# Fourier transform and feed-forward layer: the rounded products read their columns in turn from two halves

## The chip, the core and the metric

The kernel runs on one NeuronCore of a Trainium2 chip. Its engines work at the same time, each through its own list of instructions: TensorE (PE) multiplies matrices, VectorE (DVE), ScalarE (ACT) and GpSimd (POOL) work element by element, and SyncE (SP) starts transfers. They wait for each other by semaphores. SBUF is the memory on the chip, PSUM the small memory that TensorE writes its sums to; both have 128 partitions. The metric is the time of one run on the device in microseconds.

## The reference

```python
X = np.fft.fft(x, axis=1)          # x: (8, 3072, 256), real
X = np.fft.fft(X, axis=2)
x = X.real.astype(np.float32).reshape(8 * 3072, 256)
h = x @ w_in                       # (256, 2048)
g = np.maximum(h, 0.0) + alpha * np.minimum(h, 0.0)
out = g @ w_out                    # (2048, 256)
```

A transform along both axes of each of eight batches, its real part, and then a layer of 2048 features with a leaky slope for each feature, and a second layer back to 256.

## The kernel before

The feature transform is folded into the first layer's weights, and symmetries of the real transform leave half of the columns (frequencies) to compute: two output rows, i = 0 and 1, are made from each. In what follows a column is a frequency, and the features lie on the partitions.

**Products.** The bulk of the work is `nc.tensor.matmul`: a stationary operand of 128 x 128 weights, and a moving operand whose columns pass through the array. To keep float precision with a fast product, most operands are split in two rounded floats (`F32R`): hi, the rounded value, and lo, what is left. A product of such numbers is then three: hi x hi, hi x lo, lo x hi. A few products at the start (the weights, the transform's units, and the second layer of block 0 for the first 14 feature groups) are taken in plain `F32`; the profile shows two records for each of these.

**Blocks and steps.** The columns are cut in 26 blocks (`BLOCKS`): 18 of 512 columns for the batches 1 to 6, and eight of 384 or 386 for the first and last batch. Each block runs through 16 steps, one for each group of 128 features. A step `step(s)` issues, in this order on TensorE:

- `ffn1(s + 3)` (L663 to L665): two sums q = 0, 1 of three products each, moving operand `X` (the transform's result, hi and lo side by side), into two of the four PSUM banks of the ring `pq`.
- `ffn2(s)` (L742): the second layer of the step three earlier, 12 products with the moving operands hi and lo of `g`, into the four banks `acc`, which collect over the 16 steps of a block.

Beside them, `pair(s + 3)` turns the first layer's sums into the second layer's operands:

- L681, VectorE: `pf` = the sum q = 0 plus a row (frequency 128 of the features, `xbc`, loaded once a block) times a weight for each feature.
- L688, VectorE: `d` = `pf` minus or plus the sum q = 1, for the two rows i.
- L692, ScalarE: `d` times the slope, written over the sum in PSUM.
- L646, VectorE: the larger of the two, which also ends the use of the bank in `pq`.
- L648, ScalarE, and L650, GpSimd: the split of `d` into hi and lo.

**Transform.** For each next batch, `fold_piece` (L369, on GpSimd and VectorE) folds the loaded rows, spread over the steps. Then `unit` (L524, plain floats) and `dft_odd` (L480, 36 rounded products of 384 columns in a batch through `dft_parts`) multiply with cosine tables, and `to_x` writes `X`. The table of `dft_odd` is split once in six pieces by `parts` (L472, L473).

**Order.** Nothing is planned at run time: the order on each engine is that of the calls. At the end of a block `evacuate` copies the four banks `acc` to SBUF, and a transfer takes them out; the host puts the columns in their places.

## Time and profile before

| what | value |
|---|---|
| median of 3 runs | 1768.83 us (1768.09 to 1771.08) |
| the profiled execution, its span | 1770.41 us, 1768.6 us |
| TensorE busy | 1754.7 us, 99% |
| VectorE, GpSimd, ScalarE busy | 83%, 74%, 62% |
| mean granted clock of TensorE | 0.998 |
| data moved | 71.35 MB, 40 GB/s |

The span reaches from the first to the last instruction; the profiled execution's own time also holds what lies around it. A granted clock of 1.00 is the upper of TensorE's two levels, 2.4 GHz; the lower is 1.2 GHz. In the views, a matmul's record lasts longer than the distance to the next one, since products overlap in the array: distances are read from start to start. "x12" in a row of the chain or of the timeline means 12 instructions merged into one row.

### The profile page before, as it was taken

Reading aid. Unit: us, or ns where it says so; the run is one execution under the profiler, and the core shown is the slowest. Engines: PE = TensorE matmul, PEld = TensorE weight load, DVE = VectorE, ACT = ScalarE, POOL = GpSimd, SP = SyncE. Lnnn points to the kernel's source line nnn. Section 1 sums busy time; section 2 is a strip of 40 time slices with the busy share of each in tenths; the row PEclk is TensorE's granted clock in tenths of the full one; section 3 lists DMA queues with packets and bytes.
Section 4 is the critical chain, followed back from the end, with each engine's and each line's share of the span. In section 5 each row is a group of like instructions: output and inputs, shape, how many; then the busy total and the mean of one; then the engine's idle time right before and its main releaser. Section 6 shows DMA issues by size and latency. Waiting matters only on the chain.

```text
span 1768.6 us, 25521 instructions
## 1 busy us (share of the span) xinstructions
PE 1754.7 (99%) x8222; PEld 1498.3 (85%) x8222; DVE 1468.3 (83%) x2545; ACT 1105.4 (62%) x2029; POOL 1309.0 (74%) x1349
## 2 busy tenths in 40 slices
PE   8999999999999999999999999999999999999999
PEld 6789998888888888888888888888888888899998
DVE  8978987888778887888878888788877888778886
ACT  6866676555666566665665556655666556666665
POOL 2379887888678876788777887778877788666665
PEclk9999999999999999999999999999999999999999
DMA  6411120011000010010100101001100010000000
GB/s 234 147 35 44 41 67 19 19 54 49 18 31 37 31 66 1 31 48 30 55 24 7 66 13 54 24 8 65 37 30 25 18 43 29 1 29 23 23 19 19
DMA packets 26152, 71.35 MB, mean 40 GB/s; under 512 B 6272, under 2 KB 8354, under 8 KB 25890
## 3 DMA queue, kind: packets, MB, share of 16 engines
q1 hardware_dynamic: 25266, 69.27, 11.1%
q8 instruction: 64, 1.05, 0.2%
q14 instruction: 70, 0.57, 0.1%
q10 hardware_dynamic: 752, 0.45, 0.1%
HBM read 44.45 MB, written 25.25 MB: 39 GB/s over the span
## 4 chain that ended last, share of the span: by engine, by line
PE 98%; DVE 1%; POOL 0%; issue 0%; ACT 0%; DVEq 0%; POOLq 0%; ACTq 0%
PE acc L742 59%; PE pq L663 10%; PE pq L664 10%; PE pq L665 10%; PE ps L524 3%; PE ps L480 2%; PE acc L729 2%; PE ps L301 1%; PE fold L378 0%; POOL w L270 0%; PE warm L610 0%; DVE d L688 0%; DVE wm L261 0%; DVE pf L681 0%; DVE we L257 0%
## 5 line engine op out<-in xcount | busy, mean ns | idle before, releaser
L650 POOL TENSOR_TENSOR lo<-d,hi 128x512 fp32r<-128x512 f32 (+2 forms) x804 | 979.8, 1239 | 344.3 <-ACT hi L648 333.9
L648 ACT ACTIVATE hi<-d 128x512 fp32r<-128x512 f32 (+2 forms) x804 | 484.4, 603 | 486.3 <-DVE d L646 338.2
L646 DVE SCALAR_TENSOR_TENSOR d<-d,sg,pq 128x512 f32<-128x512 f32 (+2 forms) x804 | 565.1, 703 | 3.2 <-ACT pq L692 1.9
L692 ACT ACTIVATE pq<-d,sga 128x512 f32<-128x512 f32 (+2 forms) x804 | 520.3, 648 | 47.6 <-DVE d L688 47.6
L688 DVE TENSOR_TENSOR d<-pf,pq 128x512 f32<-128x512 f32 (+2 forms) x832 | 529.6, 639 | 7.8
L742 PE MATMUL acc<-hi,woh 128*128 128x512 f32 (+2 forms) x1608 | 478.1, 378 | 0.0
L681 DVE SCALAR_TENSOR_TENSOR pf<-xbc,w,pq 128x512 f32<-128x512 f32 (+2 forms) x416 | 293.2, 705 | 191.2 <-PE pq L665 188.1
L742 PE MATMUL acc<-hi,wol 128*128 128x512 f32 (+2 forms) x1608 | 418.6, 379 | 0.0
L742 PE MATMUL acc<-lo,woh 128*128 128x512 f32 (+2 forms) x1608 | 418.4, 379 | 0.0
L742 PEld LDWEIGHTS acc<-lo,woh 128*128 128x128 f32 x1608 | 297.5, 188 | 52.9
L742 PEld LDWEIGHTS acc<-hi,woh 128*128 128x128 f32 x1608 | 299.2, 188 | 50.2
L742 PEld LDWEIGHTS acc<-hi,wol 128*128 128x128 f32 x1608 | 297.8, 188 | 51.7
L663 PE MATMUL pq<-X,wih 128*128 128x512 f32 (+2 forms) x832 | 321.6, 387 | 3.3 <-DVE d L646 2.6
L664 PE MATMUL pq<-X,wih 128*128 128x512 f32 (+2 forms) x832 | 313.2, 376 | 0.2 <-DVE X L573 0.2
L665 PE MATMUL pq<-X,wil 128*128 128x512 f32 (+2 forms) x832 | 312.8, 376 | 0.0
L663 PEld LDWEIGHTS pq<-X,wih 128*128 128x128 f32 x832 | 156.6, 188 | 30.1 <-DVE d L646 4.0
L665 PEld LDWEIGHTS pq<-X,wil 128*128 128x128 f32 x832 | 156.8, 188 | 26.1 <-DVE wil L318 0.2
L664 PEld LDWEIGHTS pq<-X,wih 128*128 128x128 f32 x832 | 157.3, 189 | 24.4 <-DVE X L573 0.4
L573 POOL TENSOR_TENSOR X<-y,X 128x384 fp32r<-128x384 f32 (+3 forms) x67 | 63.9, 966 | 28.9 <-ACT X L572 28.7
L369 POOL TENSOR_TENSOR raw<-raw 128x512 f32<-128x512 f32 (+2 forms) x84 | 70.4, 838 | 0.0
L541 DVE TENSOR_TENSOR y<-ps,os 128x192 f32<-128x192 f32 (+3 forms) x76 | 23.5, 352 | 48.4 <-ACT os L531 48.4
L270 POOL TENSOR_TENSOR w<-we,wm 128x512 int32<-128x512 int32 x16 | 20.5, 1279 | 50.5 <-DVE wm L261 28.6
(155 smaller groups left out, 979.6 us busy)
## 6 DMA issues: line engine op xcount, KB each, us to landing
raw<-in_xh SPq DMA_DIRECT2D x46, 512.0 KB
out<-o SPq DMA_DIRECT2D x36, 512.0 KB
raw<-in_w SPq DMA_DIRECT2D x15, 512.0 KB
xbc<-xcd SPq DMA_DIRECT2D x18, 256.0 KB
out<-o SPq DMA_DIRECT2D x10, 386.0 KB
out<-o SPq DMA_DIRECT2D x6, 384.0 KB
odd<-in_odd SPq DMA_DIRECT2D x1, 1152.0 KB
table<-in_odd SPq DMA_DIRECT2D x6, 192.0 KB
```

The source lines that it names most:

```text
L369: yield size, lambda o=o, i0=i0, i1=i1, op=op: e.tensor_tensor(out=o, in0=i0, in1=i1, op=op)
L573: lo_engine.tensor_tensor(out=lo, in0=v, in1=hi.bitcast(F32), op=ALU.subtract)
L646: V.scalar_tensor_tensor(out=d, in0=d, scalar=sg[:, f:f + 1], in1=ad, op0=ALU.mult, op1=ALU.max)
L648: S.activation(out=hi, in_=d, func=ACTF.Copy)
L650: G.tensor_tensor(out=lo, in0=d, in1=hi.bitcast(F32), op=ALU.subtract)
L663: nc.tensor.matmul(out=t_, lhsT=wih[:, f, q], rhs=xh, start=True, stop=False)
L664: nc.tensor.matmul(out=t_, lhsT=wih[:, f, q], rhs=xl, start=False, stop=False)
L665: nc.tensor.matmul(out=t_, lhsT=wil[:, f, q], rhs=xh, start=False, stop=True)
L681: V.scalar_tensor_tensor(out=pf, in0=xbc[g], scalar=w128[:, f:f + 1], in1=ps[0], op0=ALU.mult, op1=ALU.add,)
L688: V.tensor_tensor(out=d, in0=pf, in1=ps[1], op=ALU.add if i else ALU.subtract)
L692: S.activation(out=ad, in_=d, func=ACTF.Copy, scale=sga[:, f:f + 1])
L742: nc.tensor.matmul(out=acc[o, i], lhsT=wt[:, f, o * P:(o + 1) * P], rhs=hl[i][part], start=(f == 0 and n[o] == 0), stop=(f == KF - 1 and n ...
```

## The change

Every product of rounded floats now reads its moving operand in another order: column 0, column n/2, column 1, column n/2 + 1 and so on, for n columns. The output is written to consecutive places of the PSUM bank, as before, so the sums stand there in this turned order. Two small helpers say so: `_halves` names the source in turn from its two halves, `_pairs` names the destination as consecutive pairs.

- First layer: `X` is read in turn, and the sums stand in turned order. The row `xbc` is read in turn by L681, so that it matches.
- Second layer, blocks 1 to 25: hi and lo, which stand in turned order, are read in turn once more. Block 0 stays as it is, since most of its products are plain floats. The host puts the columns back (`_turn`, once for block 0 and twice for the others).
- Odd transform: the two parts of the cosine table are written in SBUF in the inverse order, so that reading in turn gives the old order of its sums.

No instruction of computation is added, removed or moved, and no transfer. Plain-float products are as before.

```diff
+def _turn(n):
+    return np.arange(n).reshape(2, n // 2).T.reshape(-1)
+
+def _halves(v):
+    return v.rearrange("p (h a) -> p a h", h=2)
+
+def _pairs(v):
+    return v.rearrange("p (a h) -> p a h", h=2)
...
             hi, lo = (v_[:, at:at + n] for v_ in split_in[key])
+            if key == "odd":
+                v = v.rearrange("p q (a h) -> p (q a) h", h=2)
+                hi, lo = (v_.rearrange("p q (h a) -> p (q a) h", h=2) for v_ in (hi, lo))
...
-                nc.tensor.matmul(out=ps, lhsT=lhsT, rhs=rhs, start=(i == 0), stop=(i == n - 1))
+                nc.tensor.matmul(
+                    out=_pairs(ps), lhsT=lhsT, rhs=_halves(rhs), start=(i == 0), stop=(i == n - 1),
+                )
...
-            nc.tensor.matmul(out=t_, lhsT=wih[:, f, q], rhs=xh, start=True, stop=False)
-            nc.tensor.matmul(out=t_, lhsT=wih[:, f, q], rhs=xl, start=False, stop=False)
-            nc.tensor.matmul(out=t_, lhsT=wil[:, f, q], rhs=xh, start=False, stop=True)
+            xh, xl, out = _halves(xh), _halves(xl), _pairs(t_)
+            nc.tensor.matmul(out=out, lhsT=wih[:, f, q], rhs=xh, start=True, stop=False)
+            nc.tensor.matmul(out=out, lhsT=wih[:, f, q], rhs=xl, start=False, stop=False)
+            nc.tensor.matmul(out=out, lhsT=wil[:, f, q], rhs=xh, start=False, stop=True)
...
-                out=pf, in0=xbc[g], scalar=w128[:, f:f + 1], in1=ps[0], op0=ALU.mult, op1=ALU.add,
+                out=_pairs(pf), in0=_halves(xbc[g]), scalar=w128[:, f:f + 1], in1=_pairs(ps[0]),
+                op0=ALU.mult, op1=ALU.add,
...
+                out, rhs = acc[o, i], hl[i][part]
+                if g:
+                    out, rhs = _pairs(out), _halves(rhs)
                 nc.tensor.matmul(
-                    out=acc[o, i], lhsT=wt[:, f, o * P:(o + 1) * P], rhs=hl[i][part],
+                    out=out, lhsT=wt[:, f, o * P:(o + 1) * P], rhs=rhs,
```

What the built program has beyond that is waits: 384 semaphore instructions more on TensorE and 377 more on ScalarE. On TensorE, in the middle of the program, the second of a step's two first-layer sums waited for VectorE alone (a name after "waits" is the engine whose semaphore is waited for):

```order
L663 MATMUL pq<-X,wih 128x512 [waits DVE_49]
L664 MATMUL pq<-X,wih 128x512
L665 MATMUL pq<-X,wil 128x512
L663 MATMUL pq<-X,wih 128x512 [waits DVE_49]
L664 MATMUL pq<-X,wih 128x512
L665 MATMUL pq<-X,wil 128x512
```

The same place of TensorE in the changed program, whose line numbers are 21 higher there:

```order
L684 MATMUL pq<-X,wih 128x512 [waits DVE_49]
L685 MATMUL pq<-X,wih 128x512
L686 MATMUL pq<-X,wil 128x512
L684 MATMUL pq<-X,wih 128x512 [waits DVE_49,PE_49]
L685 MATMUL pq<-X,wih 128x512
L686 MATMUL pq<-X,wil 128x512
```

The products stand as before; the fourth now also waits for TensorE's own product of some 34 products earlier, the one that wrote this bank last.

## Rows read from the trace of the kernel before

**Rows 1.** The page: TensorE's busy time, and the chain that ended last by line.
```profile
PE 1754.7 (99%) x8222; PEld 1498.3 (85%) x8222; DVE 1468.3 (83%) x2545; ACT 1105.4 (62%) x2029; POOL 1309.0 (74%) x1349
...
PE acc L742 59%; PE pq L663 10%; PE pq L664 10%; PE pq L665 10%; PE ps L524 3%; PE ps L480 2%; PE acc L729 2%; PE ps L301 1%; PE fold L378 0%; POOL w L270 0%; PE warm L610 0%; DVE d L688 0%; DVE wm L261 0%; DVE pf L681 0%; DVE we L257 0%
```

**Rows 2.** Waits of TensorE: total us, times, longest.
```profile
PE pq L663 <- DVE d L646: 2.6, 4, 1.2
```

**Rows 3.** Chain of waits, steady steps: start us, us, what.
```profile
1170.72 2.80 PE acc L742 x12
...
1174.90 2.80 PE acc L742 x12
```

**Rows 4.** The same view where an odd transform stands between two layers.
```profile
287.75 3.14 PE ps L480 x18
290.89 0.24 PE pq L663
```

**Rows 5.** Timeline of TensorE at the end: start us, us, instruction; six products between.
```profile
1762.28 0.52 PE L742 MATMUL acc<-hi,wol 128*128 128x386 f32 x2
...
1763.34 0.52 PE L742 MATMUL acc<-hi,wol 128*128 128x386 f32 x2
```

**Rows 6.** Timeline of TensorE at the start, and that stretch's busy times and clock.
```profile
41.02 0.53 PE L665 MATMUL pq<-X,wil 128*128 128x386 f32 x1
...
42.31 3.40 PE L729 MATMUL acc<-gw,whole 128*128 128x386 f32 x8
...
40.00:42.30 2.30, 2.30 (x11) 2.30 (x10) 2.30 (x5) 2.21 (x5) 0.11 (x2) 0.54 0.73 228
```

**Rows 7.** Timeline of TensorE in block 0: plain-float products and what follows them.
```profile
65.59 2.76 PE L729 MATMUL acc<-gw,whole 128*128 128x386 f32 x8
68.19 1.05 PE L301 MATMUL ps<-w,feat 128*128 128x128 f32 x8
```

**Rows 8.** Groups by line and form: count | busy us, mean ns | idle before.
```profile
L742 PE MATMUL acc<-hi,woh 128*128 128x512 f32 x1152 | 360.9, 394 | 0.0
...
L663 PE MATMUL pq<-X,wih 128*128 128x512 f32 x576 | 230.3, 400 | 0.0
...
L742 PE MATMUL acc<-hi,woh 128*128 128x386 f32 x264 | 68.2, 339 | 0.0
...
L663 PE MATMUL pq<-X,wih 128*128 128x386 f32 x160 | 56.3, 352 | 1.0 <-ACT X L572 0.5 <-DVE d L646 0.5
...
L742 PE MATMUL acc<-hi,woh 128*128 128x384 f32 x192 | 49.0, 337 | 0.0
...
L663 PE MATMUL pq<-X,wih 128*128 128x384 f32 x96 | 34.9, 364 | 2.2 <-DVE d L646 2.1
...
L480 PE MATMUL ps<-oddh,col 128*128 128x384 f32 x42 | 14.1, 336 | 0.0
```

**Rows 9.** Timeline of VectorE in a steady step; idle time before in brackets.
```profile
1003.50 0.75 DVE L681 SCALAR_TENSOR_TENSOR pf<-xbc,w,pq 128x512 f32<-128x512 f32 x1 [0.57 <-PE pq L665]
1004.16 0.74 DVE L646 SCALAR_TENSOR_TENSOR d<-d,sg,pq 128x512 f32<-128x512 f32 x1
...
1006.08 0.68 DVE L688 TENSOR_TENSOR d<-pf,pq 128x512 f32<-128x512 f32 x1
1007.68 0.75 DVE L681 SCALAR_TENSOR_TENSOR pf<-xbc,w,pq 128x512 f32<-128x512 f32 x1 [0.92 <-PE pq L665]
```

**Rows 10.** Windows: a batch; us, then PE, PEld, DVE, ACT, POOL busy, PEclk, DMA.
```profile
1137.94:1350.49 212.55, 212.55 (x935) 173.91 (x935) 176.55 (x285) 130.25 (x225) 164.84 (x162) 1.00 0.10 34
```

**Rows 11.** Groups by line and form on VectorE; columns as in rows 8.
```profile
L681 DVE SCALAR_TENSOR_TENSOR pf<-xbc,w,pq 128x512 f32<-128x512 f32 x288 | 214.7, 745 | 145.7 <-PE pq L665 143.9
...
L681 DVE SCALAR_TENSOR_TENSOR pf<-xbc,w,pq 128x384 f32<-128x384 f32 x48 | 29.2, 609 | 8.8 <-PE pq L665 8.0
...
L257 DVE SCALAR_TENSOR_TENSOR we<-raw,we 128x512 int32<-128x512 int32 x15 | 10.3, 684 | 0.0
```

## The prediction, made before the changed kernel was run

> **What bounds the kernel now.** I read the page first, then the chain of waits, then TensorE alone in order of time, then VectorE beside it.

> The page says that TensorE is busy 99% of the span, and the chain that ended last is TensorE almost throughout: the second layer's rounded products (L742) hold 59%, the first layer's (L663 to L665) 30%, the odd transform (L480) 2% [rows 1]. The waits of TensorE are nearly nothing: the largest that the loop shows is 2.6 us in all [rows 2]. So there is no wait to remove. The time is the number of products times the time of one, and the reader should ask what one costs.

> A product's own duration (0.39 us) is no price, since the next begins before it ends; the price is from start to start. In the chain of waits a steady step of a 512-column block begins its second-layer products at 1170.72 and again at 1174.90: these 12 and the 6 of the first layer in 4.18 us, 232.2 ns each [rows 3]. At 2.4 GHz, the higher of the clock's two levels, 512 columns at one a clock would be 512 / 2.4 = 213.3 ns. The granted clock is 1.00 there [rows 10]. So 18.9 ns, 8.9%, is lost in every product.

> Three more readings say what kind of loss this is.
> - It grows with the columns. 18 products of 384 columns take 3.14 us, 174.4 ns each [rows 4], against 160.0: 14.4 ns, 9.0%. A price per product would have been 18.9 ns again.
> - It isn't another engine's traffic. At the very end six products of 386 columns take 1.06 us, 176.7 ns each against 160.8 [rows 5], 9.9%, when the other engines have little or nothing left to read.
> - It goes when columns are asked for at half the rate. At a granted clock of 0.54 (practically the lower level) four first-layer products of 386 columns take 1.29 us, 322.5 ns each; 386 / 1.2 is 321.7 [rows 6]. The unrounded products of block 0 at full clock take 2.59 us for eight records of 386 columns, 323.8 ns each: two clocks a column are 321.7, and 2.1 ns is left over [rows 7].

> So the array follows its clock whenever a 4-byte column is due every 0.83 ns, and falls behind, by the same share in every stage, when one is due every 0.42 ns. Either the moving operand's columns can't be fetched at that rate as they are fetched now, or the array can't take rounded columns at that rate. The change bears on the first alone: same products, same results, same instructions, another order of addresses.

> **The change part by part.** It touches 7548 products [rows 8]: 5184 of 512 columns (576 x 3 of the first layer, 1152 x 3 of the second), 1248 of 386 (160 x 3, and 264 x 3 less the 24 of block 0, which stay in order), and 1116 of 384 (96 x 3, 192 x 3, 42 x 6 of the odd transform).

> *What one product may become.* Nothing in this trace reads a moving operand with a long step between neighbouring columns, so I bound it. Best: the loss goes but for the 2.1 ns that a product keeps where columns come slowly [rows 7]: 215.4 ns for 512, 163.0 for 386, 162.1 for 384. Worst: each column takes two clocks, as in [rows 7]: 428.8, 323.8 and 322.1 ns. Between lies no change. The best end saves 5184 x 16.8 = 87.1, 1248 x 13.7 = 17.1 and 1116 x 12.3 = 13.7 us, 118 us together. The worst end adds 5184 x 196.6 + 1248 x 147.1 + 1116 x 147.7 = 1368 us.

> I take the best end. The loss is a fixed share of the columns, gone at half the demand and untouched by the neighbours: that looks like one run of addresses asked for faster than the place that holds it can answer. Two runs in turn, 1024 bytes apart at 512 columns, ask each place half as often, and half as often is what [rows 6, 7] show to be free.

> [...]

> *VectorE's sum of the first layer* (L681, 416 times) now reads its row vector from two halves in turn. The nearest row is L257: 512 words at a step of two words, 684 ns [rows 11], no longer than L646's 0.74 us on consecutive words [rows 9]. So I take nothing; the other end is each element at twice L681's own slope, (745 - 609) / 128 = 1.06 ns an element [rows 11]: 0.75 us becomes about 1.3.

> *Does VectorE keep up?* In a steady step it starts its sum at 1003.50, ends its last operation at 1006.08 + 0.68 = 1006.76 and starts again at 1007.68 [rows 9]. A step shortened to 18 x 215.4 ns = 3.88 us leaves 0.6 of those 0.9 us. Over a batch of 48 steps it works 176.5 of 212.55 us [rows 10]; TensorE would need 212.55 less 864 x 16.8 ns and 36 x 12.3 ns, 197.6 us. VectorE then stands at 89%, GpSimd (164.8) at 83%. In single steps VectorE has more (two evacuation copies, a fold operation), but its first release for the next products comes 1004.16 + 0.74 = 1004.90, 1.8 us before they start at about 1006.7. For such steps and the start I add 5 us.

> *The added waits.* 384 first-layer products wait for an earlier product of TensorE too. It stands about 34 products back, some two steps or 7 us, so it is long done; what is added is one more semaphore instruction a step in the sequencer, and the chain shows no sequencer time of TensorE. Nothing. 377 more such instructions on ScalarE fall on an engine with 130 of 212.55 us of work [rows 10]. Nothing. The table's six splits write in turn on ScalarE and GpSimd, off the path. Nothing.

> *Sum.* The profiled execution took 1770.4 us, its span 1768.6: 1.8 us outside. 1768.6 - 117.9 + 5 = 1655.7 us of span, 1657.5 with what lies around it. That execution is 1.6 us above the median of the runs (1768.83), so on the median's scale **1656 us**.

> **The rivals.**
> - *Half the loss, or VectorE takes over: 1710 us.* If two runs in turn heal only half of the loss, the saving is 59 us. The same time comes another way: with L681 at 1.3 us VectorE would need 176.5 + 48 x 0.53 = 202 us of every batch and with its gaps some 205, past TensorE's 197.6; half of the 15 us that a batch gains is lost. For it: a fixed share can have two causes. Against: L257's row.
> [...]
> - *The array itself is the limit: 1769 us.* Rounded columns at full clock cost what they cost, wherever they lie. For it: the loss is the same share for both layers' operands and the transform's. Against: nothing in the trace separates it; that it vanishes at the lower clock fits it too.

> **How the numbers follow.** The full gain has 0.42, the half gain 0.22, no effect 0.12; slower has 0.24, of which I give 0.18 to a cost far above 1800 us and 0.06 to a small one. A measurement of this kernel tells 0.2% (3.5 us) from no change. So faster 0.64, same 0.12, slower 0.24. The likeliest case alone would lie within 1646 to 1672. The range from 1645 to 1780 takes in the first three cases and the start of the slow one, and leaves out the large slowdown: 0.2.

> **What would show it.** Right: a step of 512 columns lasts about 3.88 us in the chain, the 18 products of the odd transform 2.92 us instead of 3.14, the unrounded products and the cold stretch stay as they are, and L681 stays at 0.75 us. Half: steps of 4.0 us; if TensorE then waits for VectorE's L646 it was VectorE, and if not, the fetch. [...]

## The result, and the profile after

| | before | after |
|---|---|---|
| median | 1768.46 us (4 runs) | 1662.79 us (4 runs, 1659.61 to 1664.33) |
| ratio of the runs | | 0.940, 95% interval 0.938 to 0.942 |
| span of the profiled execution | 1768.6 us | 1662.5 us |

The four runs of the kernel before are the three of its table and one more. The change makes the kernel 6.0% faster. 1656 us was forecast.

The page of the changed kernel: busy times, and the chain that ended last by line (L767 is what L742 was, L684 to L686 are the first layer, L498 the odd transform).

```profile
PE 1642.7 (99%) x8222; PEld 1475.8 (89%) x8222; DVE 1473.8 (89%) x2545; ACT 1123.8 (68%) x2029; POOL 1299.3 (78%) x1349
...
PE 93%; DVE 4%; issue 1%; ACT 0%; DMA 0%; POOL 0%; DVEq 0%; SPq 0%; POOLq 0%; ACTq 0%
PE acc L767 56%; PE pq L684 10%; PE pq L685 10%; PE pq L686 10%; PE ps L544 3%; PE ps L498 2%; PE acc L751 2%; DVE d L710 1%; DVE pf L702 1%; PE ps L316 1%; DVE d L666 1%; PE fold L393 0%; DMA raw<-in_xh 0%; DVE wm L276 0%; DVE we L272 0%
```

Where [rows 1] had hardly anything but TensorE, 4% of the chain is VectorE now. The other engines work nearly as long as before (VectorE 1473.8 us against 1468.3, ScalarE 1123.8 against 1105.4); the span around them is shorter.

The chain of waits of the changed kernel, in steady steps and at an odd transform, answers [rows 3, 4]:

```profile
284.30 2.92 PE ps L498 x18
287.22 0.22 PE pq L684
...
1102.38 2.59 PE acc L767 x12
...
1106.26 2.59 PE acc L767 x12
```

A step lasts 3.88 us where it lasted 4.18: 12 products in 2.59 us are 215.8 ns each. 18 products of 384 columns take 2.92 us, 162.2 ns. The end of the kernel, in the timeline of TensorE, answers [rows 5]; eight products begin between these two rows:

```profile
1656.30 0.49 PE L767 MATMUL acc<-hi,wol 128*128 128x386 f32 x2
...
1657.61 0.49 PE L767 MATMUL acc<-lo,woh 128*128 128x386 f32 x2
```

163.8 ns each in place of 176.7. All three widths now stand 2 to 3 ns above one column a clock at 2.4 GHz (213.3, 160.0, 160.8). Taken as one column a clock, the runs bear this figure out: from 384 to 512 columns the price rises by 53.6 ns, 0.419 ns a column or 2.39 columns in a nanosecond, and at a granted clock of 0.50 four products of 386 columns take 1.29 us (below), 1.20 columns in a nanosecond.

What did not change: the plain-float products of block 0, eight records in 2.60 us, answer [rows 7]. Nor did the products at the lower clock (granted 0.50 from 41.17 to 42.46 us): four in 1.29 us in the turned order, as in [rows 6] in the plain one. The rows of both:

```profile
63.30 2.76 PE L751 MATMUL acc<-gw,whole 128*128 128x386 f32 x8
65.90 1.05 PE L316 MATMUL ps<-w,feat 128*128 128x128 f32 x8
```

```profile
41.17 0.53 PE L686 MATMUL pq<-X,wil 128*128 128x386 f32 x1
...
42.46 3.64 PE L751 MATMUL acc<-gw,whole 128*128 128x386 f32 x8
```

A batch in the windows (columns as in [rows 10]), and VectorE's sum by form (as in [rows 11]):

```profile
1073.20:1271.10 197.90, 197.90 (x936) 174.72 (x935) 176.88 (x284) 132.59 (x225) 163.37 (x162) 1.00 0.11 37
```

```profile
L702 DVE SCALAR_TENSOR_TENSOR pf<-xbc,w,pq 128x512 f32<-128x512 f32 x288 | 218.5, 759 | 66.0 <-PE pq L686 62.9
```

The batch was forecast at 197.6 us. TensorE never stands still in it, though VectorE is busy 89%. L702 costs 759 ns in place of 745, and VectorE's idle time before it has fallen from 145.7 us to 66.0: VectorE has that much less in reserve.

The waits of TensorE (total us, times, longest) show what is new:

```profile
PE pq L684 <- DVE d L666: 6.5, 9, 2.3
...
PE pq L685 <- POOL X L911: 1.8, 1, 1.8
```

The first was 2.6 us [rows 2]. Its longest, 2.30 us, stands in the first batch behind a fold operation on VectorE, of the kind that the 5 us of the forecast were meant for:

```profile
180.45 3.52 DVE L384 TENSOR_TENSOR xev<-raw 128x512 f32<-128x512 f32 x1 [0.20 <-DMA raw<-in_xh]
...
185.08 0.43 PE L684 MATMUL pq<-X,wih 128*128 128x384 f32 x1 [2.30 <-DVE d L666]
```

The second did not exist before, and the timeline of the changed kernel shows it in block 0:

```profile
60.15 0.41 PE L684 MATMUL pq<-X,wih 128*128 128x386 f32 x1
...
61.00 1.26 POOL L285 TENSOR_TENSOR w<-we,wm 128x512 int32<-128x512 int32 x1 [2.21 <-DVE wm L276]
...
62.20 0.13 POOL L911 MEMSET X<- 128x28 f32 x1
...
62.38 0.43 PE L685 MATMUL pq<-X,wih 128*128 128x386 f32 x1 [1.83 <-POOL X L911]
```

A product waits for the clearing of seven columns of `X`, which stands behind GpSimd's work on the weights. The product reads columns 0 to 385, the clearing is at 1537: they share nothing. But with the turned order the built program lets the clearing wait for TensorE and the product for the clearing. It is the first layer's order that does it: in `e8_second_only` below, where the first layer reads `X` in plain order, this wait is not in the list.

### The profile page after: what moved, and what is told of

The parts are those of the page before. It is cut to its first block, busy times and chain, and to the rows that moved or that the text cites. A ratio compares the mean times of both kernels' runs of the same rounds, so it can differ in the third digit from the quotient of the medians.

```text
span 1662.5 us, 26282 instructions
## 1 busy us (share of the span) xinstructions
PE 1642.7 (99%) x8222; PEld 1475.8 (89%) x8222; DVE 1473.8 (89%) x2545; ACT 1123.8 (68%) x2029; POOL 1299.3 (78%) x1349
## 4 chain that ended last, share of the span: by engine, by line
PE 93%; DVE 4%; issue 1%; ACT 0%; DMA 0%; POOL 0%; DVEq 0%; SPq 0%; POOLq 0%; ACTq 0%
PE acc L767 56%; PE pq L684 10%; PE pq L685 10%; PE pq L686 10%; PE ps L544 3%; PE ps L498 2%; PE acc L751 2%; DVE d L710 1%; DVE pf L702 1%; PE ps L316 1%; DVE d L666 1%; PE fold L393 0%; DMA raw<-in_xh 0%; DVE wm L276 0%; DVE we L272 0%
## 5 line engine op out<-in xcount | busy, mean ns | idle before, releaser
L714 ACT ACTIVATE pq<-d,sga 128x512 f32<-128x512 f32 (+2 forms) x804 | 526.3, 655 | 48.9 <-DVE d L710 48.1
L767 PE MATMUL acc<-hi,woh 128*128 128x512 f32 (+2 forms) x1608 | 454.1, 364 | 0.0
L767 PE MATMUL acc<-lo,woh 128*128 128x512 f32 (+2 forms) x1608 | 393.1, 364 | 0.0
L767 PE MATMUL acc<-hi,wol 128*128 128x512 f32 (+2 forms) x1608 | 393.1, 364 | 0.0
L702 DVE SCALAR_TENSOR_TENSOR pf<-xbc,w,pq 128x512 f32<-128x512 f32 (+2 forms) x416 | 298.3, 717 | 92.6 <-PE pq L686 87.6
L767 PEld LDWEIGHTS acc<-hi,woh 128*128 128x128 f32 x1608 | 298.0, 189 | 31.0
L767 PEld LDWEIGHTS acc<-lo,woh 128*128 128x128 f32 x1608 | 295.3, 189 | 30.9
L767 PEld LDWEIGHTS acc<-hi,wol 128*128 128x128 f32 x1608 | 295.3, 189 | 30.9
L684 PE MATMUL pq<-X,wih 128*128 128x512 f32 (+2 forms) x832 | 310.7, 373 | 7.1 <-DVE d L666 6.5
L685 PE MATMUL pq<-X,wih 128*128 128x512 f32 (+2 forms) x832 | 302.6, 364 | 2.0 <-POOL X L911 1.8
L686 PE MATMUL pq<-X,wil 128*128 128x512 f32 (+2 forms) x832 | 302.5, 364 | 0.0
L684 PEld LDWEIGHTS pq<-X,wih 128*128 128x128 f32 x832 | 157.6, 189 | 26.9 <-PE pq L686 4.1
L686 PEld LDWEIGHTS pq<-X,wil 128*128 128x128 f32 x832 | 157.6, 189 | 15.7 <-DVE wil L333 0.3
```

Source lines behind the costliest of these rows:

```text
L684: nc.tensor.matmul(out=out, lhsT=wih[:, f, q], rhs=xh, start=True, stop=False)
L685: nc.tensor.matmul(out=out, lhsT=wih[:, f, q], rhs=xl, start=False, stop=False)
L686: nc.tensor.matmul(out=out, lhsT=wil[:, f, q], rhs=xh, start=False, stop=True)
L702: V.scalar_tensor_tensor(out=_pairs(pf), in0=_halves(xbc[g]), scalar=w128[:, f:f + 1], in1=_pairs(ps[0]), op0=ALU.mult, op1=ALU.add,)
L714: S.activation(out=ad, in_=d, func=ACTF.Copy, scale=sga[:, f:f + 1])
L767: nc.tensor.matmul(out=out, lhsT=wt[:, f, o * P:(o + 1) * P], rhs=rhs, start=(f == 0 and n[o] == 0), stop=(f == KF - 1 and n[o] == 2),)
```

## The experiments

The result leaves open why the order heals. Theory A: a column must not lie in the same 16 bytes as the one before it. Theory B: two runs far apart are needed. That 16 bytes is the size that counts was an assumption at this point; `e2_near16` and `e9_near8` bear on it. The first four runs change the order in the 18 blocks of 512 columns alone: `_halves` and `_pairs` get another pattern there, and the host puts the columns back accordingly. The narrow blocks and the odd transform stay in turn from two halves. Each later cut of `_halves` shows its line against the first run's; `_pairs` follows it, so that the output of each product stays in consecutive places, and so does the host's `_turn`, but for `e7_each_twice`. In `e2_near16`, `e3_lines`, `e6_twos`, `e7_each_twice` and `e9_near8` the sum on VectorE reads its row in plain order, so the row is not at its columns there; the products are as many and as large as before. From each run the steady step in the chain of waits is shown: twelve products of the second layer, and the next twelve 18 products later.

**A step of 16 bytes** (`e1_step4`).

```diff
 def _halves(v):
+    if v.shape[-1] == WM:
+        return v.rearrange("p (a h) -> p h a", h=4)
     return v.rearrange("p (h a) -> p a h", h=2)
 def _pairs(v):
+    if v.shape[-1] == WM:
+        return v.rearrange("p (h a) -> p h a", h=4)
     return v.rearrange("p (a h) -> p a h", h=2)
```

> Blocks of 512 columns read columns 0, 4, 8, ... and then 1, 5, 9, ...: one ascending run with a step of 16 bytes, so that no two columns in a row lie within the same 16 bytes. The narrow blocks and the odd transform stay in turn from two halves. Theory A (the same 16 bytes asked twice in a row are slow; any order that avoids it heals): 215.8 ns a product of 512 columns, as in the changed kernel, 1663 us in all. Theory B (two runs far apart are needed): 232 ns or more, 5184 x 16.4 ns = 85 us above the changed kernel, 1748 us. [...]

2938.53 us. The chain:

```profile
912.34 5.54 PE acc L770 x12
920.65 5.54 PE acc L770 x12
```

8.31 us for 18: 462 ns a product, twice the time of plain order. Theory A falls at once: no two columns in a row share 16 bytes. The slowdown is larger than the prediction's worst end (428.8); the halves, at 215.8, don't meet it.

**In turn from two places 16 bytes apart** (`e2_near16`).

```diff
-        return v.rearrange("p (a h) -> p h a", h=4)
+        return v.rearrange("p (b h a) -> p b a h", h=2, a=4)
```

> Blocks of 512 columns read 0, 4, 1, 5, 2, 6, 3, 7 and so on: in turn from two places 16 bytes apart, all within one ascending run of eight columns. The sum with the row of frequency 128 (L702) reads its row in plain order, so that row stands at other columns than it should. Theory A: 215.8 ns, 1663 us. Theory B: 232 ns, 1748 us. [...]

1661.18 us. The chain:

```profile
901.40 2.59 PE acc L770 x12
905.29 2.59 PE acc L770 x12
```

215.8 ns, as with the halves 1024 bytes apart: theory B falls.

**Four columns from one half, four from the other** (`e3_lines`).

```diff
-        return v.rearrange("p (a h) -> p h a", h=4)
+        return v.rearrange("p (h b a) -> p b h a", h=2, a=4)
```

> Blocks of 512 columns read 0, 1, 2, 3 and then 256, 257, 258, 259 and so on: 16 bytes from one half, then 16 bytes from the other. L702 reads its row in plain order, as in the run before. Theory A: three of four columns in a row lie within the same 16 bytes as before the change, so 232 ns and 1748 us. Theory B: 215.8 ns, 1663 us. [...]

1850.66 us. The chain:

```profile
903.10 3.03 PE acc L770 x12
907.65 3.03 PE acc L770 x12
```

253 ns, more than in plain order (the later expectations have it as 252). Two far runs alone don't heal; in this order they cost 21 ns more than plain order. A's 232 is off as well.

**A step of 8 bytes** (`e4_step2`): the pattern of the first run with h=2.

> Blocks of 512 columns read 0, 2, 4, ... and then 1, 3, 5, ...: one ascending run with a step of 8 bytes, two columns from each 16 bytes. Theory A: of the pairs of columns in a row half lie within the same 16 bytes, in place of three quarters, so two thirds of the loss of 16.4 ns stay: 226.7 ns, 1719 us. Theory B: 232 ns, 1748 us. [...]

2890.66 us. The chain:

```profile
912.76 5.44 PE acc L770 x12
920.92 5.44 PE acc L770 x12
```

453 ns, where the theories said 227 and 232. Both have failed. What orders the six numbers is to look at every other place of the stream: the columns at its even places, and those at its odd places. In plain order the even places are 0, 2, 4, 6: two columns from each 16 bytes. In the halves and in `e2_near16` they are 0, 1, 2, 3: four. With a step of two they are 0, 4, 8, with a step of four 0, 8, 16: one. Four cost 215.8 ns, two 232 to 253, one 453 to 462. That is theory R of the next runs. Its two readers, each of which holds a piece, are a picture made for this count: the runs show the prices, not the readers.

**In turn from four quarters** (`e5_quarters`): `"p (h a) -> p a h"` with h=4.

2010.92 us. The chain:

```profile
907.34 3.40 PE acc L770 x12
912.44 3.40 PE acc L770 x12
```

**Two columns from each half in turn** (`e6_twos`): `"p (h b a) -> p b h a"` with h=2, a=2.

> Blocks of 512 columns read 0, 1, 256, 257, 2, 3, 258, 259 and so on: two columns from each half in turn. L702 reads its row in plain order. Theory R: the even places are 0, 256, 2, 258, so each reader changes its piece at every column: about 455 ns a product and 2900 us. Theory H: the two pieces in use are both held, each serves its four columns: 215.8 ns and 1660 us, at most 252.

2241.35 us. The chain:

```profile
907.71 3.92 PE acc L770 x12
913.60 3.92 PE acc L770 x12
```

283 and 327 ns. Both are far slower than plain order, as R has it and A (215.8 for the quarters) and H (215.8 to 252 for the twos) have not; but R's 455 missed both, and H's 455 the quarters. It may be that going to and fro between pieces and coming back to them costs less than leaving them for good; no run tests that by itself. R has the direction right for such orders, and their size wrong.

**Each column twice** (`e7_each_twice`).

```diff
-        return v.rearrange("p (a h) -> p h a", h=4)
+        return v[:, 0:256].rearrange("p (a h) -> p a h", h=1).to_broadcast([P, 256, 2])
```

> Blocks of 512 columns read 0, 0, 1, 1, 2, 2 and so on: the first half of the columns, each twice; the second half is left out of the products (and of the output). L702 reads its row in plain order. Theory R: each reader takes 0, 1, 2, 3 and so on, four columns from each piece, so 215.8 ns a product and 1660 us, though both readers are always in the same 16 bytes. Theory A: neighbours in the stream always share 16 bytes, so 232 ns or more and 1748 us. Theory H: 215.8 ns.

1659.51 us. The chain:

```profile
903.63 2.59 PE acc L770 x12
907.52 2.59 PE acc L770 x12
```

215.8 ns, with the even and the odd places always in the same 16 bytes. So a shared piece is no obstacle, and A is out for good. The order also reads half as many different bytes, so for R alone it is weaker evidence than the next run.

**In turn from two places 8 bytes apart** (`e9_near8`).

```diff
-        return v.rearrange("p (a h) -> p h a", h=4)
+        return v.rearrange("p (b h a) -> p b a h", h=2, a=2)
```

> Blocks of 512 columns read 0, 2, 1, 3, 4, 6, 5, 7 and so on: in turn from two places 8 bytes apart. L702 reads its row in plain order. Theory R in the form that the second four runs leave (each of two readers takes every other column, and what counts is how many columns 16 bytes give it before it goes elsewhere): the even places are 0, 1, 4, 5, 8, 9, so two columns from each 16 bytes, as in plain order: about 232 ns a product and 1748 us. Rival U (the unit is 8 bytes, or any second place heals): 215.8 ns and 1660 us.

1744.65 us. The chain:

```profile
900.93 2.80 PE acc L770 x12
905.11 2.80 PE acc L770 x12
```

4.18 us for 18, 232 ns: exactly plain order's price, as R says, where the even places are 0, 1, 4, 5. This run does what the change does, but within four columns, and gains nothing. Together with `e2_near16`, where the only difference is eight columns in place of four, it puts the unit at 16 bytes: with pieces of 8 or of 32 bytes R would have given both runs the same price. It also settles a rival from the output: the sums are written as consecutive pairs here as in the change, and nothing is gained, and `e6_twos`, with the same output, takes 327 ns.

**The second layer alone** (`e8_second_only`).

```diff
-            xh, xl, out = _halves(xh), _halves(xl), _pairs(t_)
+            out = t_
...
-                out=_pairs(pf), in0=_halves(xbc[g]), scalar=w128[:, f:f + 1], in1=_pairs(ps[0]),
+                out=pf, in0=xbc[g], scalar=w128[:, f:f + 1], in1=ps[0],
```

> The change only in the second layer and the odd transform; the first layer's products and L702 read in plain order. All theories: the second layer's products at 215.8 ns, the first layer's at 230 to 234. Against the kernel before, 3456 x 16.4 ns of the 512-column products, 1344 x 13 ns of the narrow ones and 252 x 12 ns of the odd transform, 77 us, so about 1691 us; the first layer's part of the gain is the other 28 us or so. If the gain hung on both operands' order at once, this run would be at 1768.

1694.33 us, 3 us above the expectation. The chain has both prices side by side, first-layer products at the old 0.23 us and second-layer products at 2.59 us for twelve:

```profile
908.28 0.23 PE pq L684
...
909.68 2.59 PE acc L767 x12
```

The gain is paid product by product; neither part needs the other.

**The new wait** (`e10_again`, `e11_early`, on one chip with nine runs of the kernel before). The first is the changed kernel as it was; the cut is the second's.

```diff
+    G.memset(X[:, :, X0 + SINGLE:X0 + SINGLE + 7].bitcast(F32), 0.0)
     unit_store(0, "see", 0, G, y)
...
                 if r == 3:
-                    G.memset(X[:, :, X0 + SINGLE:X0 + SINGLE + 7].bitcast(F32), 0.0)
```

> The changed kernel once more, as the one that the next run is measured against: a ratio to the kernel before of 0.940.

> The changed kernel with the clearing of seven columns of X (line 911 there) issued before the first unit of the transform is stored, in place of step 3. In the changed kernel a first-layer product at 62.38 us waits 1.83 us for that clearing, which itself waits for TensorE; the kernel before had no such wait. Theory: that wait goes, and 2 us with it, 0.1%: ratio 0.939. Rival: the 2 us are given back at the next wait of TensorE for VectorE in the first batch, and nothing changes.

The changed kernel once more: 1665.00 us, ratio 0.9406 (0.9393 to 0.9419). With the early clearing: 1660.71 us, 0.9388 (0.9375 to 0.9401). The waits of TensorE in the latter:

```profile
PE ps L316 <- POOL w L285: 6.3, 4, 2.6
PE pq L684 <- DVE d L666: 5.6, 7, 2.3
```

The wait for the clearing is gone and the wait for VectorE has not grown (6.5 us in both profiles of the changed kernel). The wait for the weights (6.3 us) was 4.4 and 6.6 us in these two, so it moves by as much from one execution to the next, and one trace can't show that nothing was given back. The version's best estimate is 4 us below the changed kernel, but the two intervals overlap; that it is faster is likely, not shown. Of the versions that compute the whole it has the lowest median.

## Why the prediction was right, point by point

- *The loss is in the fetch of columns, not in the array.* Right, and now shown: the same products in other orders take 215.8 to 462 ns, where a limit of the array would have left them alike.
- *The whole loss goes.* Right. Taken against the prices before, the products save 5184 x (232.2 - 215.8) = 85.0, 1248 x (176.7 - 163.8) = 16.1 and 1116 x (174.4 - 162.2) = 13.6 us, 114.7 of the 117.9 forecast. The 2.1 ns that a product was to keep are about 2.5. (The eight records of [rows 7] take 2.60 us, not 2.59; that makes 3.3 ns, and a hundredth of a microsecond in the reading is 1.3 ns.)
- *Why it goes.* Wrong. "Two runs in turn ... ask each place half as often" is theory B, and `e3_lines` (two runs far apart, 253 ns) and `e2_near16` (one run, 215.8 ns) refute it. The size came out since the limit was taken from rows that held whatever the reason. That the order reached this limit was luck as far as the argument goes: by the same argument four quarters in turn, which ask each place a quarter as often, should have healed too, and they take 283 ns.
- *The worst end, and the 0.18 for a cost far above 1800 us.* No row of the kernel before tells how likely such a cost was, and this change met none of it (215.8 ns). Other orders of the same products do: two clocks a column were put at 428.8 ns, and the steps of 16 and 8 bytes take 462 and 453 (2938.53 and 2890.66 us). Counted over every other place of the stream, one column from each 16 bytes costs that much, two cost 232 in plain order and four 215.8. The sizes of the quarters (283) and the twos (327) the count doesn't give.
- *VectorE keeps up.* Right in the batches, 197.9 us against 197.6. L702 rose by 14 ns, not by 0.5 us. With another order it would have been close: at the 1165 ns that this sum takes in `e1_step4` (below) VectorE would have some 196 us of work in a batch of 197.9, an estimate from 176.9 and 48 times 0.41 us.
- *The added waits cost nothing.* Wrong in one place. The waits looked at were the counted ones, of TensorE for itself and of ScalarE, and they show no cost in the batches; the one new wait of TensorE for GpSimd, for the clearing, cost 1.8 us and was missed.
- *5 us for single steps and the start.* Too little. The span fell by 106.1 us, so of the 114.7 some 9 were given back, and all of it in the first batch. The 18 products of the odd transform that [rows 4] have at 287.75 us stand at 284.30 in the changed kernel, 3.45 us earlier, where the 96 products of 386, 864 of 384 and 36 of 512 columns before them should have saved 12.4. From there to the end nothing more is lost, so the 176.7 ns, taken for all products of 386 columns and used most in the last batch, were no bad price. Of these 9 us 1.8 are the clearing's and 3.9 more are in TensorE's waits for VectorE; the other 3 lie in the same stretch and are not placed more exactly. The 3.9 are not surely all the change's: for this wait the rows by form give 4.0 us in `e4_step2` (0.6 and 3.4), the list 6.5 in the changed kernel, and the first batch of these two is the same. So of the 7 us by which the forecast was short, some 3 are the product's price and some 4 this term.

Open: what the parity is physically. The two readers were a picture formed from the first six orders, and no run shows them by themselves; of the four orders tried after it, two came out in size (each column twice, 8 bytes) and two in kind only (the quarters, the twos). And why two columns from each 16 bytes cost 232 ns in plain order but 253 when the pieces lie far apart was not tried further.

## What to carry to other kernels

Where one engine is busy 99%, compare the distance from start to start of its instructions with what the clock allows, at two sizes and at both clock levels: a share that grows with the columns and goes at half the demand may be a feed, and an order of addresses may heal it; only a run with another order tells it from a limit of the array. For a rounded-float product as in this kernel, take the moving operand so that every other column of the stream stays in the same 16 bytes four times in a row (two halves in turn, or columns 0, 4, 1, 5 and so on); all such orders tried here take 215.8 ns for 512 columns, against 232.2 in plain order, with the output in consecutive places. Another output was not tried. When an access pattern changes, read the list of waits again on all engines: with a pattern that has a step the build may add waits between accesses that share nothing.

## What the runs showed of the hardware that was not expected

- A moving operand of 4-byte columns with a step of 8 or 16 bytes takes 453 and 462 ns for 512 columns, against 232 in plain order: the first is hardly cheaper, though it goes to a new piece of 16 bytes half as often.
- VectorE too pays for some orders, but not for the same ones. Its sum L705 with the row at a step of 16 bytes, and from four quarters in turn, by line and form:

```profile
L705 DVE SCALAR_TENSOR_TENSOR pf<-xbc,w,pq 128x512 f32<-128x512 f32 x288 | 335.6, 1165 | 1034.6 <-PE pq L689 1034.5
```

```profile
L705 DVE SCALAR_TENSOR_TENSOR pf<-xbc,w,pq 128x512 f32<-128x512 f32 x288 | 324.2, 1126 | 268.6 <-PE pq L689 268.5
```

  It costs 1165 and 1126 ns against 745 in plain order, but only 759 from two halves in turn, and 747 with a step of 8 bytes (`e4_step2`), where TensorE takes twice its time.
- ScalarE's split of the cosine table, which now writes in turn at 768 bytes' distance, went from 509 to 887 ns (six times; the chain of waits does not pass through it):

```profile
L490 ACT ACTIVATE oddh<-table 128x384 fp32r<-128x384 f32 x6 | 5.3, 887 | 0.0
```
